# K and V laid out and fetched two heads at a time in a fused block-sparse attention and MoE kernel

## The chip, the cores and the metric

The kernel runs on one core of one Trainium2 chip. The metric is the device time of one execution, in microseconds (us). Of the kernel before three runs were timed: 549.1 us median (547.7 to 552.0).

## The reference

Attention over 4 batches, 8 heads, 768 tokens and 64 columns a head, in blocks of 32 tokens: a query block sees its neighbours, the first and the last block, and three blocks drawn at random for it (`sampled_blocks`). The first and last query blocks see everything. A top-1 mixture of 8 experts follows.

```python
scores = scale * np.matmul(q, k.transpose(0, 1, 3, 2))       # masked to window, first, last, sampled blocks
attn = np.exp(scores - max); attn = attn / (sum + 1e-9)
x = np.matmul(attn, v) -> (3072 tokens, 512)
e = argmax(x @ w_gate);  out = gate * sigmoid(x @ w_output_gate)[e] * (relu(x @ w1[e]) @ w2[e])
```

## The kernel before

The four batches are taken two at a time ("pairs of batches", `bp` 0 and 1): the two batches lie in the two halves of the partitions. One pass over a pair has `PER` = 26 steps. The first 4 steps are **dense** (class `Dense`): the first and the last query block of two heads (`u` and `u + 4`), against all 24 blocks of K. The 22 steps behind are **sparse** (class `Sparse`): 11 pairs of query blocks times two groups of four heads. The first experts' units run beside the second pass, the others after it.

K of one pair of batches is held as `kn`, 24 blocks of 256 columns (8 heads of 32 tokens), V as `vn`, six pieces of 128 tokens with all heads. For a pair of query blocks a tile `kr` (three in turn) collects 12 scaled K blocks: two copied by POOL once per `kr` (`fixed`, L410), four by DVE (`window_k`, L438), six drawn by number (`gather_k`, L421), of which ACT copies one and POOL five. Drawn V rows come by indirect DMA from POOL (`gather_v`, L448) with the row list `vidx`.

A step `n` runs, in program order on PE: the scores `pS` of step n, the output `pO` of step n-2 and the transposes `pT` of step n-1. DVE takes the row maxima (`dM`), ACT the exponentials (`aE`). A dense `pS` of step n+1 writes the score banks which the exponentials of step n read.

What else is to be issued is entered with `at(step, rank, function)` and runs at that step, in order of rank; each engine executes strictly in the order written. `spread` holds an SP transfer of ranks 3.3 and 3.6 in the first pass back to the step's first maximum or first ACT copy. The transfers of SP and ACT use eight semaphores in turn, so a transfer is issued only when the one eight before it has landed.

At the start PE runs warm-up matmuls on constants (`warm`, L172; their counts are in `NWARM`) until K is there. SP fetches the list of drawn blocks (`raw`, L193), K in two transfers of 12 blocks each (L395), V in six (L398), and then queries, V rows and gate weights. POOL and DVE make from `raw` the row list `vidx` (`setup_dup`, `setup_blocks`). A table in DRAM, by which experts find their tokens, is filled with a constant in four transfers (`fill`, L370) from a tile that POOL sets at step 3 (`setup_rest`). K of the second pair comes in 12 transfers (`LOAD_K`), its V in six (`LOAD_V`).

In the second pass SP also fetches expert weights in pieces of 512 KB (`load_w`, L983), which ACT (L1068) and DVE (L1072) split into two halves, and POOL gathers the tokens of the first units (`load_x`, L1010), which PE transposes (L1040).

Of the kernel before, what the change touches and what calls it, by code (L numbers as in the profile page):

```python
# [83 lines left out]
LOAD_K = 4, 5, 7, 9, 11, 13, 15, 17, 19, 21, 22, 23  # L84
# [17 lines left out]
NWARM = 44, 21, 11, 8, 8  # L102
# [16 lines left out]
def tile_kernel(ctx, tc, q, k, v, sampled, wg, wcat, out):  # L119
# [202 lines left out]
    def setup_blocks():  # L322
# [37 lines left out]
        nc.vector.tensor_copy(vidx[:, 1], tab)  # L360

    def setup_rest():
# [4 lines left out]
        for f in range(4):  # L367
            at(cur[0] + f, 3.3, fill, f, tz)
# [13 lines left out]
    vc = [ring.tile([128, 2, 8, VW], F32, name=f"vc{i}") for i in range(RC)]  # L382
# [38 lines left out]
    def gather_k(bp, i, kind, ns):  # L421
# [5 lines left out]
        for n, rv in zip(ns, regs):  # L427
            slot = n + 4 if n < 3 else n - 2
            if kind == "dve":
                nc.vector.tensor_single_scalar(r[:, slot:slot + 1], kn[bp][:, ds(rv, 1)], EXPS, op=ALU.mult)  # L430
            elif kind == "act":
                nc.scalar.activation(r[:, slot:slot + 1], kn[bp][:, ds(rv, 1)], AF.Copy, scale=EXPS)
            else:
                nc.gpsimd.tensor_tensor(  # L434
                    r[:, slot], kn[bp][:, ds(rv, 1)].rearrange("p o n -> p (o n)"), eighth.to_broadcast([128, 256]),
                    op=ALU.mult)

    def window_k(bp, i):  # L438
        a = 1 + 2 * i
        r = kr[i % RK]  # L440
        nc.vector.tensor_single_scalar(r[:, 0], kn[bp][:, a + 2], EXPS, op=ALU.mult)
        nc.vector.tensor_single_scalar(r[:, 7:10], kn[bp][:, a - 1:a + 2], EXPS, op=ALU.mult)

    def window_v(bp, i):
        a = 769 * bp + 32 + 64 * i
        spread(nc.sync.dma_start(vc[i % RC][0:64].rearrange("p b j w -> p (b j w)"), v[a:a + 64]))

    def gather_v(bp, i, s):  # L448
        if s == 0:
            vt[bp, i] = ring.tile([128, 2, 2, 8, VW], F32, tag="vt", name=f"vt{bp}_{i}", bufs=RV)  # L450
        behind(nc.gpsimd.indirect_dma_start(  # L451
            vt[bp, i][:, s].rearrange("p b j w -> p (b j w)"), None, v,
# [54 lines left out]
    class Sparse:  # L507
# [7 lines left out]
        def pS(self):  # L515
# [5 lines left out]
            for hp in range(2):  # L521
                for h2 in range(2):
                    for qi in range(2):
                        for b in range(2):
                            j = 4 * h2 + 2 * hg + hp
                            p = slice(64 * b, 64 * b + 64)
# [3 lines left out]
                                g[p, 1 - qi:3:1 + qi, :, 32 * j:32 * j + 32], start=True, stop=True)  # L530
# [19 lines left out]
        def pO(self):  # L550
# [3 lines left out]
            for b in range(2):  # L554
                for hp in range(2):
                    for h2 in range(2):
                        for qi in range(2):
# [4 lines left out]
                                av[:, qi, b, 4 * h2 + 2 * hg + hp], start=b == 0 and hp == 0, stop=False)  # L562
            for b in range(2):
                for hp in range(2):
                    for h2 in range(2):
# [954 lines left out]
```

## Time and profile before

| | |
|---|---|
| median of 3 runs | 549.1 us (547.7 to 552.0) |
| profiled execution, its own time | 543.43 us |
| its span | 541.8 us |
| busy share of PE, DVE, ACT, POOL | 94%, 66%, 57%, 46% |
| mean granted TensorE clock | 0.991 |

Times in rows are microseconds from the start of the span. PE is TensorE's matmuls, PEld its weight loads, DVE VectorE, ACT ScalarE, POOL GpSimd, SPq and POOLq the instructions that issue transfers. `[3.67 <-DMA x]` says that the engine was idle for 3.67 us before this instruction and what ended the idleness. The profiled execution is 5.7 us shorter than the median of the timed runs.

### The profile page before, as it was taken

What the parts mean: (1) busy time and instruction counts of PE and PEld (TensorE: products, weight loads), DVE (VectorE), ACT (ScalarE), POOL (GpSimd) and SP (SyncE); (2) the same over time, 40 slices, a digit from 0 to 9 for tenths busy, and PEclk for the clock granted to TensorE, in tenths of its full rate; (3) what the DMA queues carried; (4) which work ended last, traced back from release to release, by engine and by line L of the source; (5) the groups of instructions that cost most, each with busy time, mean ns of one, the idle gap of its engine ahead of it and who ended that gap; (6) DMA issues with size and microseconds to landing.
All of it is one profiled execution on the core that took longest, in us unless ns stands there. A gap on an engine that the chain in (4) does not pass through costs nothing. (4 is left out here: it accounts for less than half of the span.)

```text
span 541.8 us, 18874 instructions
## 1 busy us (share of the span) xinstructions
PE 510.1 (94%) x7429; PEld 358.9 (66%) x7429; DVE 357.3 (66%) x732; ACT 311.5 (57%) x584; POOL 249.0 (46%) x369
## 2 busy tenths in 40 slices
PE   8999999988879999999999999999999999999993
PEld 5466676666557667776777766677666667676671
DVE  5568577585679766876876668776755754465580
ACT  1455666665666656776666555666562663554480
POOL 3466566752755855548646337553421503211120
PEclk9999999999998999999999999999999999999997
DMA  7969988889399769887767595599998999996111
GB/s 295 280 197 306 294 259 264 237 239 298 92 327 311 202 224 301 242 230 251 220 209 227 142 343 197 203 391 402 405 301 299 325 399 313 301 326 232 28 40 37
DMA packets 60062, 137.98 MB, mean 255 GB/s; under 512 B 20471, under 2 KB 27131, under 8 KB 59708
## 3 DMA queue, kind: packets, MB, share of 16 engines
q1 hardware_dynamic: 48524, 99.93, 57.0%
q0 software_dynamic: 11296, 36.49, 21.1%
q8 instruction: 60, 0.98, 0.7%
q10 hardware_dynamic: 144, 0.26, 0.2%
q14 instruction: 38, 0.31, 0.2%
HBM read 127.88 MB, written 14.81 MB: 263 GB/s over the span
## 5 line engine op out<-in xcount | busy, mean ns | idle before, releaser
L1086 PE MATMUL h<-xb,kr 128*128 128x256 f16 (+1 forms) x780 | 86.9, 261 | 1.4 <-DMA xb<-xb 1.4
L1118 PE MATMUL S<-kr,hh 128*128 128x512 f16 x348 | 85.4, 379 | 0.0
L1086 PEld LDWEIGHTS <-kr 128*128 128x128 f16 x780 | 69.5, 98 | 19.7 <-issue 2.8
L434 POOL TENSOR_TENSOR kr<-kn,eighth 128x256 f32<-128x256 f32 x110 | 68.7, 651 | 9.1 <-issue 7.1
L534 DVE TENSOR_REDUCE mx<-S 128x4 f32<-128x1024 f32 x44 | 53.7, 1219 | 28.1 <-PE S L527 16.6
L542 ACT ACTIVATE P<-S,mx 128x256 f32<-128x256 f32 x176 | 69.1, 484 | 1.1 <-DVE mx L534 1.0
L451 POOL DMA_INDIRECT vt<-in_v_dram,vidx x44 | 45.0, 1022 | 51.5 <-DVE den L504 29.0
L1118 PEld LDWEIGHTS <-hh 128*128 128x128 f16 x384 | 36.9, 98 | 30.4
L493 ACT COPY pt<-T 128x512 f32<-128x512 f32 x66 | 36.9, 592 | 31.0 <-PE T L490 28.6
L1099 ACT ACTIVATE hh<-h 128x512 f16<-128x512 f32 (+1 forms) x36 | 19.7, 548 | 55.9 <-PE h L1086 55.4
L1010 POOL DMA_INDIRECT xb<-xscr,tab x16 | 20.7, 1295 | 63.0 <-issue 23.6
L527 PE MATMUL S<-kr,qall 64*32 64x256 f32 x1408 | 49.5, 386 | 0.0
L490 PE MATMUL T<-ident,P 128*128 128x128 f32 x352 | 46.0, 274 | 0.0
L1072 DVE SCALAR_TENSOR_TENSOR kr<-e,kr 128x1024 f16<-128x1024 f32 x32 | 38.3, 1219 | 9.8 <-ACT kr L1068 9.8
L804 POOL DMA_INDIRECT table<-vals,place x24 | 26.7, 1114 | 33.1 <-DVE den L504 21.1
L490 PEld LDWEIGHTS T<-ident,P 128*128 128x128 f32 x352 | 40.1, 143 | 1.6 <-issue 1.3
L560 PE MATMUL O<-vt,pt 128*32 128x65 f32 x1408 | 32.8, 222 | 4.7 <-issue 4.1
L1105 DVE SCALAR_TENSOR_TENSOR hh<-h,hh 128x512 f16<-128x512 f32 (+1 forms) x36 | 22.5, 626 | 19.7 <-ACT hh L1099 16.6
L1072 DVE SCALAR_TENSOR_TENSOR ws<-e,ws 128x1024 f16<-128x1024 f32 x24 | 29.9, 1246 | 7.0 <-PE h L1086 4.3
L560 PEld LDWEIGHTS O<-vt,pt 128*32 128x32 f32 x1408 | 25.6, 110 | 13.0 <-issue 8.8
L1086 PEld LDWEIGHTS <-ws 128*128 128x128 f16 x324 | 29.9, 99 | 5.4 <-issue 0.4
L1068 ACT ACTIVATE kr<-e 128x1024 f16<-128x1024 f32 x32 | 33.1, 1050 | 0.0
(349 smaller groups left out, 972.5 us busy)
## 6 DMA issues: line engine op xcount, KB each, us to landing
e<-in_wcat_dram SPq DMA_DIRECT2D x80, 512.0 KB
rk<-in_wcat_dram SPq DMA_DIRECT2D x30, 512.0 KB
vc<-in_wcat_dram SPq DMA_DIRECT2D x14, 512.0 KB
vn<-in_v_dram SPq DMA_DIRECT2D x12, 520.0 KB
xscr<-x SPq DMA_DIRECT2D x48, 128.0 KB
qall<-in_q_dram SPq DMA_DIRECT2D x23, 256.0 KB
vc<-in_v_dram SPq DMA_DIRECT2D x22, 260.0 KB
ws<-in_wcat_dram SPq DMA_DIRECT2D x8, 512.0 KB
```

The source lines that it names most:

```text
L434: nc.gpsimd.tensor_tensor(r[:, slot], kn[bp][:, ds(rv, 1)].rearrange("p o n -> p (o n)"), eighth.to_broadcast([128, 256]), op=ALU.mult)
L451: behind(nc.gpsimd.indirect_dma_start(vt[bp, i][:, s].rearrange("p b j w -> p (b j w)"), None, v, bass.IndirectOffsetOnAxis(ap=vidx[:, bp, ...
L490: nc.tensor.transpose(pt[:, 128 * c:128 * c + 128], p[:, 128 * c:128 * c + 128], ident)
L493: mark("copy", nc.scalar.copy(t[:, 0:w], pt[:, 0:w]))
L527: nc.tensor.matmul(s[64 * h2 + 32 * qi:64 * h2 + 32 * qi + 32, b, hp], t[p, 64 * j + 32 * qi:64 * j + 32 * qi + 32], g[p, 1 - qi:3:1 + qi, ...
L534: mark("max", nc.vector.tensor_reduce(mx, self.s.rearrange("p b h n -> p (b h) n"), axis=AX.X, op=ALU.max, negate=True))
L542: nc.scalar.activation(p[:, 256 * hp:256 * hp + 256], self.s[:, b, hp], AF.Exp, bias=self.mx[:, 2 * b + hp:2 * b + hp + 1])
L560: nc.tensor.matmul(o[row:row + 32, b, hp, 0:VW], self.t[b][:, col:col + 32], av[:, qi, b, 4 * h2 + 2 * hg + hp], start=b == 0 and hp == 0, ...
L1068: nc.scalar.activation(w[:, 0], piece(n), AF.Copy, scale=SW)
L1072: nc.vector.scalar_tensor_tensor(w[:, 1], piece(n), SW, w[:, 0], op0=ALU.mult, op1=ALU.subtract)
L1086: nc.tensor.matmul(hps[n // 2][:, cols(n)], w[:, hl, 128 * c:128 * c + 128], x[:, xl, c], start=cnt == 0, stop=cnt == 11)
L1118: nc.tensor.matmul(y, a[:, k], w[:, l, 512:1024], start=n % 8 == 0 and cnt == 0, stop=n % 8 == 7 and cnt == 2)
```

## The change

The columns of K are reordered in DRAM and in `kn`: the slowest index is now the pair of heads `u`, u + 4 (four "parts"), then the block, then 64 columns. V's rows are reordered in the same way. K of the first pair of batches comes in four transfers of one part each (768 KB), and the first of them stands ahead of `raw` on SP. V comes in twelve: the two first parts of all six pieces, then, behind the last part of K, the two others. Copies of single K blocks read or write four runs of 64 columns.

`setup_blocks` becomes a generator of four pieces, which run before step 0 and in steps 0, 1 and 2. `tz` is set on POOL before step 0, and the table's fills stand at steps 2 and 3. 30 of the warm-up matmuls with 512 columns go (one group of 11, and 19 of another's 21); the two groups of 8 in step 1 stay. The 12 transfers of the second K go to other steps, now by part and 8 blocks. In the second pass the fixed V rows (`fixed_v`) stand at steps 3, 5, 7 of the pass instead of 2, 3, 4, and the weight pieces of the first unit are fetched one step later.

```diff
-LOAD_K = 4, 5, 7, 9, 11, 13, 15, 17, 19, 21, 22, 23
+LOAD_K = 3, 3, 4, 5, 13, 15, 17, 19, 20, 21, 22, 23
-NWARM = 44, 21, 11, 8, 8
+NWARM = 44, 2, 8, 8
...
         for f in range(4):
-            at(cur[0] + f, 3.3, fill, f, tz)
+            at(2 + f // 2, (3.3, 3.6)[f % 2], fill, f, tz)
...
-    def load_k(bp, c):
-        spread(nc.sync.dma_start(kn[bp][:, c], k[bp, :, c]))
+    def load_k(bp, u, c):
+        spread(nc.sync.dma_start(
+            kn[bp][:, u, c].rearrange("p c x -> p (c x)"), k[bp, :, u, c].rearrange("p c x -> p (c x)")))
...
+    def parts(t):
+        return t.rearrange("p (u x) -> p u x", u=4)
...
             else:
                 nc.gpsimd.tensor_tensor(
-                    r[:, slot], kn[bp][:, ds(rv, 1)].rearrange("p o n -> p (o n)"), eighth.to_broadcast([128, 256]),
-                    op=ALU.mult)
+                    parts(r[:, slot]), block(bp, rv), eighth.unsqueeze(2).to_broadcast([128, 4, 64]), op=ALU.mult)
...
-        nc.vector.tensor_single_scalar(r[:, 7:10], kn[bp][:, a - 1:a + 2], EXPS, op=ALU.mult)
+        nc.vector.tensor_single_scalar(
+            r[:, 7:10].rearrange("p c (u x) -> p u c x", u=4), kn[bp][:, :, a - 1:a + 2], EXPS, op=ALU.mult)
...
                         nc.tensor.matmul(
                             self.s[b][64 * h2:64 * h2 + 64, half, 0:384], t[p, 64 * j:64 * j + 64],
-                            kn[bp][p, 12 * half:12 * half + 12, 32 * j:32 * j + 32], start=True, stop=True)
+                            kn[bp][p, u, 12 * half:12 * half + 12, 32 * h2:32 * h2 + 32], start=True, stop=True)
...
     load_q(0, NPAIR)
+    load_k(0, 0, slice(0, NB))
     setup_load()
     setup_dup()
-    load_k(0, slice(0, 12))
-    load_k(0, slice(12, 24))
+    load_k(0, 1, slice(0, NB))
+    load_k(0, 2, slice(0, NB))
...
     for c in range(6):
-        load_v(0, c)
+        load_v(0, c, slice(0, 2))
+    load_k(0, 3, slice(0, NB))
+    for c in range(6):
+        load_v(0, c, slice(2, 4))
...
-    setup_blocks()
+    blocks = setup_blocks()
+    next(blocks)
+    for n in range(3):
+        at(n, 3, next, blocks)
+    setup_rest()
...
-    at(3, 3, setup_rest)
...
-            at(o + (3 if bp == 0 else 2) + r, 3, fixed_v, bp, r)
+            at(o + (3 + r if bp == 0 else 3 + 2 * r), 3, fixed_v, bp, r)
...
-                    do(max(p - 5, (-3, 5, 5, 15)[u]), 0.6, load_w, n)
+                    do(max(p - (5 if u else 4), (-3, 5, 5, 15)[u]), 0.6, load_w, n)
```

How the change moves instructions. SP's queue from its first transfer on, before:

```order
L193 DMA raw<-in_sampled_dram 128x144
L395 DMA kn_224<-in_k_dram 128x3072 x2
L398 DMA vn_225<-in_v_dram 128x1040 x6
L404 DMA qall<-in_q_dram 128x512
L417 DMA vc_206<-in_v_dram 32x1040 x2
```

and with the change:

```order
L401 DMA kn_205<-in_k_dram 128x1536
L193 DMA raw<-in_sampled_dram 128x144
L401 DMA kn_205<-in_k_dram 128x1536 x2
L406 DMA vn_206<-in_v_dram 128x520 x6
L401 DMA kn_205<-in_k_dram 128x1536
L406 DMA vn_206<-in_v_dram 128x520 x6
L414 DMA qall<-in_q_dram 128x512
L430 DMA vc_187<-in_v_dram 32x1040 x2
```

The first part of K now goes ahead of the list of blocks, the last part goes behind half of V.

DVE's queue at the first two dense steps, with the change (before, all the rows on `sf`, `t`, `wf`, `tab` and `vidx` stood ahead of the first maximum; `mx0d_0` is the first maximum of step 0, `pt0d_0` a copy of its transposes):

```order
L336 SCALAR_TENSOR_TENSOR bad<-dd,bad 128x72
L616 TENSOR_REDUCE mx0d_0_293<-S_75 128x1
L616 TENSOR_REDUCE mx1d_0_295<-S_76 128x1
L340 TENSOR_SCALAR sf<-sf,rf 128x72
L344 TENSOR_TENSOR sf<-sf,t_277 128x72
L616 TENSOR_REDUCE mx1d_1_330<-S_76 128x1
L511 COPY pt1d_0_342<-T1d_0_338 128x384
L349 CAST wf<-wi 128x22
L350 TENSOR_SCALAR wf<-wf,rf 128x22
L456 TENSOR_SCALAR kr_184<-kn_205 128x256
L457 TENSOR_SCALAR kr_184<-kn_205 128x4x3x64
L616 TENSOR_REDUCE mx0d_2_449<-S_75 128x1
```

(Rows between them are left out.) The third piece of the lists stands between the copies of step 0 and the window's copies into `kr`, which stand ahead of step 2's maximum.

SP's queue at the start of the second pass, before (`e` are weight pieces, `vc` V rows):

```order
L987 DMA e_3450<-in_wcat_dram 128x1024
L417 DMA vc_206<-in_v_dram 32x1040 x2
L446 DMA vc_206<-in_v_dram 64x1040
L404 DMA qall<-in_q_dram 128x512
L987 DMA e_3450<-in_wcat_dram 128x1024
L417 DMA vc_207<-in_v_dram 32x1040 x2
```

and with the change:

```order
L1002 DMA e_3428<-in_wcat_dram 128x1024
L462 DMA vc_187<-in_v_dram 64x1040
L414 DMA qall<-in_q_dram 128x512
L1002 DMA e_3428<-in_wcat_dram 128x1024
L430 DMA vc_187<-in_v_dram 32x1040 x2
```

Ahead of the first row stand two more weight pieces before and one with the change; the fixed V rows (32x1040, two at a time) go behind the next weight piece.

## Rows read from the trace of the kernel before

**Rows 1.** The page's first part: busy time, share of the span, instructions.
```profile
PE 510.1 (94%) x7429; PEld 358.9 (66%) x7429; DVE 357.3 (66%) x732; ACT 311.5 (57%) x584; POOL 249.0 (46%) x369
```

**Rows 2.** Waits of PE: engine, line, waited for; us in total, times, longest.
```profile
PE O L1040 <- DMA e<-xscr,tab: 2.9, 2, 2.0
```

**Rows 3.** Timeline of the first 35 us, all engines: start, us, engine, line.
```profile
1.72 9.56 PE L175 MATMUL O<-ones,ones 128*128 128x128 f16 x65 [1.72 <-DVE eighth L181]
...
6.45 0.63 ACT L408 ACTIVATE qall<-qall 128x512 f32<-128x512 f32 x1 [3.67 <-DMA qall<-in_q_dram]
6.62 0.19 DVE L323 COPY smp<-raw 1x72 int32<-1x72 int32 x1 [3.24 <-DMA raw<-in_sampled_dram]
...
7.04 0.27 POOL L229 TENSOR_TENSOR dupd<-dupf 128x48 f32<-128x48 f32 x1
...
7.38 0.27 POOL L230 TENSOR_TENSOR dupd<-dupd 128x48 f32<-128x48 f32 x1
...
7.92 0.23 DVE L336 SCALAR_TENSOR_TENSOR bad<-dd,bad 128x72 f32<-128x72 f32 x1
...
10.14 0.17 DVE L347 CAST wf<-wi 128x22 f32<-128x22 int32 x1
...
11.63 0.17 DVE L355 COPY tab<-sf 32x11 f32<-32x11 f32 x1
...
12.60 0.18 DVE L360 CAST vidx<-tab 128x22 int32<-128x22 f32 x1
...
14.04 0.61 POOL L412 TENSOR_TENSOR kr<-kn,eighth 128x256 f32<-128x256 f32 x1 [3.03 <-DMA kn<-in_k_dram]
...
15.42 0.96 DVE L601 TENSOR_REDUCE mx0d<-S 128x1 f32<-128x768 f32 x1 [2.64 <-PE S L593]
...
19.48 1.19 POOL L412 TENSOR_TENSOR kr<-kn,eighth 128x256 f32<-128x256 f32 x2
...
22.95 0.55 DVE L442 TENSOR_SCALAR kr<-kn 128x768 f32<-128x768 f32 x1
...
23.37 1.52 PE L593 MATMUL S<-kn,qall 64*64 64x384 f32 x16
...
25.00 0.96 DVE L601 TENSOR_REDUCE mx0d<-S 128x1 f32<-128x768 f32 x1 [1.49 <-ACT kr L432]
...
30.15 0.96 DVE L601 TENSOR_REDUCE mx0d<-S 128x1 f32<-128x768 f32 x1 [1.58 <-PE S L593]
...
33.65 1.09 PE L527 MATMUL S<-kr,qall 64*32 64x256 f32 x32
```

**Rows 4.** Stretches: busy us of each engine, then granted clock, DMA share, GB/s.
```profile
0.00:6.45 6.45, 4.74 (x45) 4.84 (x46) 2.27 (x20) 1.49 (x2) 2.43 (x17) 1.00 0.54 161
0.00:8.25 8.25, 6.54 (x52) 5.60 (x53) 3.82 (x29) 2.11 (x3) 3.73 (x23) 1.00 0.64 219
0.00:14.04 14.04, 12.32 (x83) 7.95 (x84) 7.11 (x48) 2.11 (x3) 5.27 (x28) 1.00 0.78 300
0.00:17.85 17.85, 15.82 (x101) 9.07 (x102) 8.93 (x50) 3.56 (x7) 8.23 (x33) 1.00 0.83 325
```

**Rows 5.** Stretches later on; columns PE, PEld, DVE, ACT, POOL as above.
```profile
55.00:60.00 5.00, 3.71 (x100) 2.83 (x99) 2.22 (x6) 3.08 (x8) 3.04 (x4) 1.00 1.01 309
160.50:162.85 2.35, 0.32 (x4) 0.11 (x2) 2.28 (x7) 2.12 (x5) 0.00 (x0) 1.00 1.02 279
164.00:167.30 3.30, 3.30 (x68) 2.49 (x54) 3.22 (x6) 1.05 (x2) 1.92 (x3) 0.51 1.03 263
```

**Rows 6.** Timeline at the start of the second pass.
```profile
153.13 0.99 POOL L1010 DMA_INDIRECT e<-xscr,tab  x1 [0.72 <-DVE dend L504]
...
162.85 0.63 PE L1040 MATMUL O<-ident,e 128*128 128x128 f32 x4 [2.04 <-DMA e<-xscr,tab]
...
171.10 0.97 DVE L442 TENSOR_SCALAR kr<-kn 128x768 f32<-128x768 f32 x1
```

**Rows 7.** Groups of instructions: line, engine, shapes, count, busy us, mean ns.
```profile
L434 POOL TENSOR_TENSOR kr<-kn,eighth 128x256 f32<-128x256 f32 x110 | 68.7, 651 | 9.1 <-issue 7.1 <-PE S L527 1.3
```

More of the change, by code (lines that the diff above doesn't have):

```diff
@@ L351, in setup_blocks @@
         for g in range(4):
+            if g == 2:
+                yield
             pp = slice(32 * g, 32 * g + 32)
@@ L360, in setup_blocks @@
         nc.vector.tensor_copy(vidx[:, 1], tab)
+        yield
     def setup_rest():
@@ L381, in tile_kernel @@
     kr = [ring.tile([128, 12, 256], F32, name=f"kr{i}") for i in range(RK)]
-    vc = [ring.tile([128, 2, 8, VW], F32, name=f"vc{i}") for i in range(RC)]
+    vc = [ring.tile([128, 4, 2, 2, VW], F32, name=f"vc{i}") for i in range(RC)]
     qall = ring.tile([128, RQ, 512], F32, name="qall")
@@ L388, in prep_alloc, with load_v @@
     def prep_alloc(bp):
-        kn[bp] = big.tile([128, NB, 256], F32, tag="kn", name=f"kn{bp}", bufs=2)
+        kn[bp] = big.tile([128, 4, NB, 64], F32, tag="kn", name=f"kn{bp}", bufs=2)
     def prep_alloc_v(bp):
-        vn[bp] = big.tile([128, 6, 2, 8, VW], F32, tag="vn", name=f"vn{bp}", bufs=1)
-    def load_k(bp, c):
-        spread(nc.sync.dma_start(kn[bp][:, c], k[bp, :, c]))
-    def load_v(bp, c):
-        spread(nc.sync.dma_start(vn[bp][:, c].rearrange("p b j w -> p (b j w)"), v[769 * bp + 128 * c:769 * bp + 128 * c + 128]))
+        vn[bp] = big.tile([128, 6, 4, 2, 2, VW], F32, tag="vn", name=f"vn{bp}", bufs=1)
+    def load_k(bp, u, c):
+        spread(nc.sync.dma_start(
+            kn[bp][:, u, c].rearrange("p c x -> p (c x)"), k[bp, :, u, c].rearrange("p c x -> p (c x)")))
+    def load_v(bp, c, us=slice(0, 4)):
+        n = VROW // 4
+        spread(nc.sync.dma_start(
+            vn[bp][:, c, us].rearrange("p u b h w -> p (u b h w)"),
+            v[769 * bp + 128 * c:769 * bp + 128 * c + 128, n * us.start:n * us.stop]))
     qt, vt = {}, {}
@@ L412, in fixed @@
             nc.gpsimd.tensor_tensor(
-                kr[r][:, 10 + j], kn[bp][:, 23 * j], eighth.to_broadcast([128, 256]), op=ALU.mult)
+                parts(kr[r][:, 10 + j]), kn[bp][:, :, 23 * j], eighth.unsqueeze(2).to_broadcast([128, 4, 64]), op=ALU.mult)
     def fixed_v(bp, r):
@@ L440, in window_k @@
         r = kr[i % RK]
-        nc.vector.tensor_single_scalar(r[:, 0], kn[bp][:, a + 2], EXPS, op=ALU.mult)
-        nc.vector.tensor_single_scalar(r[:, 7:10], kn[bp][:, a - 1:a + 2], EXPS, op=ALU.mult)
+        nc.vector.tensor_single_scalar(parts(r[:, 0]), kn[bp][:, :, a + 2], EXPS, op=ALU.mult)
+        nc.vector.tensor_single_scalar(
+            r[:, 7:10].rearrange("p c (u x) -> p u c x", u=4), kn[bp][:, :, a - 1:a + 2], EXPS, op=ALU.mult)
     def window_v(bp, i):
         a = 769 * bp + 32 + 64 * i
-        spread(nc.sync.dma_start(vc[i % RC][0:64].rearrange("p b j w -> p (b j w)"), v[a:a + 64]))
+        spread(nc.sync.dma_start(vc[i % RC][0:64].rearrange("p u b h w -> p (u b h w)"), v[a:a + 64]))
     def gather_v(bp, i, s):
         if s == 0:
-            vt[bp, i] = ring.tile([128, 2, 2, 8, VW], F32, tag="vt", name=f"vt{bp}_{i}", bufs=RV)
+            vt[bp, i] = ring.tile([128, 2, 4, 2, 2, VW], F32, tag="vt", name=f"vt{bp}_{i}", bufs=RV)
         behind(nc.gpsimd.indirect_dma_start(
-            vt[bp, i][:, s].rearrange("p b j w -> p (b j w)"), None, v,
+            vt[bp, i][:, s].rearrange("p u b h w -> p (u b h w)"), None, v,
             bass.IndirectOffsetOnAxis(ap=vidx[:, bp, i, s:s + 1], axis=0)).ins)
@@ L529, in pS @@
                                 t[p, 64 * j + 32 * qi:64 * j + 32 * qi + 32],
-                                g[p, 1 - qi:3:1 + qi, :, 32 * j:32 * j + 32], start=True, stop=True)
+                                g[p, 1 - qi:3:1 + qi, :, n:n + 32], start=True, stop=True)
         def dM(self):
@@ L561, in pO @@
                                 o[row:row + 32, b, hp, 0:VW], self.t[b][:, col:col + 32],
-                                av[:, qi, b, 4 * h2 + 2 * hg + hp], start=b == 0 and hp == 0, stop=False)
+                                av[:, qi, 2 * hg + hp, b, h2], start=b == 0 and hp == 0, stop=False)
             for b in range(2):
@@ L568, in pO @@
                             o[64 * h2:64 * h2 + 64, b, hp, 0:VW], self.t[b][:, col:col + 64],
-                            cv[:, b, 4 * h2 + 2 * hg + hp], start=False, stop=b == 1 and hp == 1)
+                            cv[:, 2 * hg + hp, b, h2], start=False, stop=b == 1 and hp == 1)
         def fin(self):
@@ L628, in pO @@
                             o[64 * h2:64 * h2 + 64, b, 0, 0:VW], t[:, col + 64 * h2:col + 64 * h2 + 64],
-                            vn[bp][:, c, b, 4 * h2 + u], start=b == 0 and c == 0, stop=b == 1 and c == 5)
+                            vn[bp][:, c, u, b, h2], start=b == 0 and c == 0, stop=b == 1 and c == 5)
         def fin(self):
@@ L931, in piece @@
             pool4["k"] = big.tile([128, 6, 1024], F32, tag="kn", name="rk", bufs=2)
-        v = [t.rearrange("p b j w -> p (b j w)")[:, 0:1024] for t in vc]
+        v = [t.rearrange("p u b h w -> p (u b h w)")[:, 0:1024] for t in vc]
         a, b = early_buffers(0), early_buffers(1)
@@ L1408, in tile_kernel @@
         if step == 1:
-            warm(3, 512)
+            warm(2, 512)
         enters = isinstance(now, Dense) and isinstance(last, Sparse)
@@ L1423, in tile_kernel @@
                 if step == 1:
-                    warm(4, 512)
+                    warm(3, 512)
                 now.aE()
```

25 lines of the change are left out of this document (14 added, 11 removed).

## Prediction

> **What bounds the kernel now.** First the page: PE is busy 94% of the span [rows 1], so what the kernel loses it loses where PE has no work. The waits of PE name only one large transfer, the gathered tokens of the second pass [rows 2]. But at the start the warm-up matmuls count as work: 65 of them run back to back from 1.72 us [rows 3], and they compute nothing. So the second view is the timeline of the first 35 us. There the first row maximum starts at 15.42, at the end of DVE's wait for the scores [rows 3], and the scores had waited for K, whose second half POOL has at 14.04 [rows 3]. Until then the transfers bound the kernel. Third, the stretches: how much has been moved by when, and where else PE idles. [...]
>
> **When a transfer lands.** By 6.45 us 161 GB/s x 6.45 = 1.04 MB have moved, and q and `raw` (262 and 74 kB) have landed [rows 3, 4]: 0.70 MB more than they hold. By 14.04 it is 300 x 14.04 = 4.21 MB, for q, `raw` and all of K (3.48 MB): 0.73 more [rows 3, 4]. So I take a transfer as landed when 0.72 MB more than it and those ahead of it have moved. K's first part (786 kB) behind q: 0.26 + 0.79 + 0.72 = 1.77 MB; at 8.25 us 219 x 8.25 = 1.81 MB [rows 4], so **8.2 us**. `raw` comes 0.2 us later, at 8.4 instead of 6.6. The second part: 10.2. The last part, behind half of V: q, `raw`, four parts and 1.60 MB of V are 5.08 MB, with 0.72 it is 5.80; at 17.85 us 325 x 17.85 = 5.80 [rows 4], so **17.85 us**. The second half of V: 1.6 MB later, below 22.
>
> **The change, part by part.**
>
> *First scores.* q is on ACT's queue and now shares the engines with K's first part instead of the small `raw`. It lands between its own 6.45 and 8.2, and 0.63 us of scaling [rows 3] follow: 7.1 to 8.9, I take 8.5. The 16 matmuls of a dense step take 1.52 us [rows 3], so they end at 10.0. DVE's first list piece, 6.62 to 8.15 [rows 3], runs from 8.4 to 10.0 and is just out of the way. The first maximum starts at 10.1 instead of 15.42: **5.3 us earlier** (4.9 to 6.7). The second part of K (10.2) is there when the exponentials free the banks, the third at about 12.
>
> *Warm-ups.* The 30 matmuls cost nothing: PE waits for K there. Their cover gone, PE idles from about 7 (45 matmuls are done by 6.45, one or two remain [rows 4]) to 8.5.
>
> *Lists on DVE.* The second piece (five operations) fits between the maxima of steps 0 and 1, as POOL's part of the list, 1.8 us later with `raw`, is done by 11.5. The third piece, 10.14 to 11.63, so 1.5 us [rows 3], stands between step 0's copies and the window copies. DVE's idle time ahead of step 2's maximum is 1.49 us [rows 3], so it just fits. The fourth piece (11.63 to 12.78, 1.15 us) goes into a gap of 1.58 [rows 3]. So the lists alone cost about 0. But the window's two copies need K's last part (17.85), and POOL, which did its copies from 14.04 to 20.67 beside a mostly idle DVE [rows 3], now does them from 17.85 on, beside the window's. The large window copy takes 0.55 us at 22.95 [rows 3] and 0.97 at 171.10 beside POOL's copies [rows 6]: 0.42 for it, about 0.2 for the small one. I take **0.6 us later** (0.2 to 1.4: the upper end if the last part of K comes at the 309 GB/s of [rows 5] from 14.04 on, at 19.2). [...]
>
> *POOL.* Its copies end 6.6 us [rows 3] after 17.85, at 24.5, those for the first sparse step before that. That step started at 33.65 [rows 3] and would now start at 29: 4.5 us to spare. The setting of the table's tile moves ahead of them, into POOL's wait for K; 0. The row list is ready at about 25, when POOL reaches the gather of V rows; 0.
>
> *Copies in four runs.* The shapes' sizes stay; 0, see the last rival.
>
> *Table, second K.* Four fills (1.77 MB) leave the stretch from 32 to 49 us for about 20 to 28, when SP's queue stood still before; four K pieces are fetched by step 5. So there is less traffic from 35 to 65, where PE idled 1.29 us in five [rows 5]. I take **0.5 us gained** (0 to 1.3). SP's row for the fill now waits for step 2's maximum, with only later transfers behind it; 0.
>
> *Second pass.* The gather of tokens issued at 153.13 holds PE until 162.85 [rows 6], 9.7 us, with the engines full. Ahead of it or beside it, one weight piece (524 kB) and four fixed V transfers (532 kB) go later: 1.06 MB, 3.8 us at 279 GB/s [rows 5], of which the gather's queue gets a part. PE's wait is 2.04, and half of 3.3 us at the lower clock is 1.65 [rows 2, 5]; so at most 3.7 us. But DVE is busy 2.28 of the 2.35 us of this wait [rows 5] and comes late next. I take **1.0 us gained** (0 to 3.7). Pieces of weights that come a step later have over 12 us between transfer and use.
>
> *Sum.* -5.3 + 0.6 - 0.5 - 1.0 = **-6.2 us**. The profiled execution took 543.4 us by its own time (span 541.8), so 537.2 by this sum. The median of the timed runs is 549.1, 5.7 us higher for reasons that this profile cannot show; taking the same 6.2 off gives **542.9 us**.
>
> **Rivals.**
>
> *The second pass gives all.* If PE's wait and the clock's fall both go (3.7), the middle gives 1.3 and the start 4.9, it is 9.9: **539**. For it: the transfers are full there; against: DVE is too. Chance 0.10.
>
> *Half the lead is lost at the start.* The first part of K lands near 9.5 (the early rate of the rows is the least sure number), or PE, now idle from 7, drops to the lower clock: then the 1.52 us of step 0 and those of step 1 take twice as long, some 3 us. 2.5 to 3.5 us less: **545.5**. For it: an idle 2.35 us preceded the fall in [rows 5]. Against it: the gap here is some 1.5 us. [...] Chance 0.20.
>
> *POOL's late start eats it.* POOL begins 3.8 us later than before (17.85 against 14.04). If the sparse steps hang on its queue, copies and gathers of V rows in turn, only 0 to 2 us are left: **548.5** (546.5 to 550.5). Against it: the 4.5 us to spare. Chance 0.11.
>
> *POOL's copies get slower: the other side.* 110 copies at 651 ns [rows 7] now read and write four runs of 64 instead of one of 256. POOL is busy 3.04 of 5 us [rows 5], some 2.4 of it such copies, so it is full when a copy takes 1.8 times as long, 1.2 us. From there each 0.1 us costs 110 x 0.1 = 11 us: at 1.35 us it is 16 - 6, so **559**. Against it: on POOL 24 runs of 2 numbers took 0.27 us, as much as 48 in one run [rows 3]. Chance 0.07.
>
> That the change does not do what it says is out: each part of K is a transfer of its own, and by the order of instructions the first scores wait for one.
>
> **How the numbers follow.** My forecast, 5 to 7.7 us less, has 0.52; 541.4 to 544.1. A measurement of this kernel tells 1%, 5.5 us, from no change: faster means below 543.6, slower above 554.6. Of the forecast 0.42 lies below 543.6, with the first rival's 0.10 this is 0.52 for faster. Same: 0.10 + 0.20 + 0.11 = 0.41. Slower: 0.07. The range reaches from 538.5, the first rival, to 548.5; it leaves out the last rival and half of the one before it.
>
> **What would show it.** In the profile after: the first maximum near 10.1 us (if at 12, the rate or the clock); K's last part on POOL at 17.9; step 2's maximum near 20.3; the first sparse scores near 29.0; POOL's copies still near 651 ns; PE's wait for the gathered tokens under 1 us and no fall of the clock at 160. If the first sparse scores start before 29.5 and the time is still above 545, the later terms are wrong: the lead was given back, and PE's waits must name the place.

## The result, and the profile after

| | kernel before | with the change | ratio, 95% interval |
|---|---|---|---|
| first comparison, 4 runs each | 549.6 us | 542.9 us | 0.9894 (0.9850 to 0.9938) |
| second, another chip, 35 and 12 runs | 537.0 | 535.9 | 0.9983 (0.9945 to 1.0021) |
| third, another chip, 35 and 12 runs | 548.8 | 543.7 | 0.9918 (0.9885 to 0.9951) |
| fourth, another chip, 35 and 12 runs | 548.9 | 544.7 | 0.9941 (0.9906 to 0.9976) |

The first row is the result that the forecast stood against: 542.9 us, as forecast. The other three came with the experiments. Times the median, the ratios are 5.8 us less (3.4 to 8.2), 0.9 (-1.1 to 3.0), 4.5 (2.7 to 6.3) and 3.2 (1.3 to 5.2); the mean of the four is 3.6. Three of the four intervals exclude 1, so the change makes the kernel faster, but by less than the sum's 6.2 us: only the first comparison lies in the forecast range of 5 to 7.7 us less. The ratios, and the mean times and clocks below, leave out runs more than 1.5% longer than the fastest of their kernel; the medians take in all.

The two profiles at hand cannot show this: the span is 541.5 us after and was 541.8 before. The profiled execution of before (543.43 us) is quicker than every one of the 74 timed runs of it in the comparisons where its median is 548.8 us or more. So stretches are compared below, not ends. First the page after, to be set beside [rows 1, 7].

```profile
span 541.5 us, 18824 instructions
...
PE 504.1 (93%) x7399; PEld 356.2 (66%) x7399; DVE 359.0 (66%) x732; ACT 311.9 (58%) x584; POOL 249.2 (46%) x369
...
DMA  8999889897299689878776594699998999996111
...
L450 POOL TENSOR_TENSOR kr<-kn,eighth 128x256 f32<-128x256 f32 x110 | 70.2, 665 | 7.4 <-issue 6.8
```

PE has 30 matmuls less, and POOL's copies take 665 ns in place of 651. The start, timelines of PE, then DVE, then POOL (start, us, engine, line):

```profile
6.92 1.52 PE L608 MATMUL S<-kn,qall 64*64 64x384 f32 x16
...
11.40 2.46 PE L608 MATMUL S<-kn,qall 64*64 64x384 f32 x16 [1.13 <-ACT P01d L625]
...
29.05 1.09 PE L544 MATMUL S<-kr,qall 64*32 64x256 f32 x32
```
```profile
7.87 0.18 DVE L323 COPY smp<-raw 1x72 int32<-1x72 int32 x1 [4.49 <-DMA raw<-in_sampled_dram]
...
9.31 0.95 DVE L616 TENSOR_REDUCE mx0d<-S 128x1 f32<-128x768 f32 x1
...
18.78 0.97 DVE L457 TENSOR_SCALAR kr<-kn 128x768 f32<-128x768 f32 x1
19.67 0.95 DVE L616 TENSOR_REDUCE mx0d<-S 128x1 f32<-128x768 f32 x1
...
23.10 0.61 DVE L360 COPY tab<-sf 32x11 f32<-32x11 f32 x1
23.73 0.56 DVE L359 COPY tab<-wf 32x11 f32<-32x11 f32 x1
```
```profile
18.72 1.50 POOL L425 TENSOR_TENSOR kr<-kn,eighth 128x256 f32<-128x256 f32 x2 [7.06 <-DMA kn<-in_k_dram]
```

The scores start at 6.92, right behind the warm-ups and without a wait, so K's first part had landed by then, at least 1.3 us before the forecast landing. They end at 8.44; the first maximum waits until 9.31 behind the list's first piece, which `raw` releases only at 7.87. It was at 15.42 [rows 3]. Step 2's maximum is at 19.67, the first sparse scores start at 29.05 (33.65 before): the lead is 4.6 us, as the sum had it by there.

Further on, the stretches of 21 to 56 us, before and then after (columns as in [rows 4]):

```profile
21.00:28.00 7.00, 6.67 (x86) 4.04 (x84) 5.37 (x11) 5.30 (x11) 0.00 (x0) 1.00 0.65 116
...
35.00:42.00 7.00, 6.60 (x145) 5.33 (x140) 4.74 (x11) 2.34 (x7) 6.05 (x33) 1.00 0.91 265
42.00:49.00 7.00, 6.19 (x164) 4.63 (x165) 6.04 (x21) 5.12 (x13) 3.58 (x5) 1.00 0.98 317
```
```profile
21.00:28.00 7.00, 4.95 (x78) 3.25 (x76) 6.80 (x17) 3.83 (x9) 6.64 (x11) 1.00 1.07 274
...
35.00:42.00 7.00, 7.00 (x167) 5.84 (x169) 6.31 (x21) 3.25 (x8) 5.19 (x8) 1.00 1.04 247
42.00:49.00 7.00, 4.76 (x130) 3.27 (x126) 5.05 (x13) 3.58 (x10) 3.27 (x5) 1.00 1.03 333
```

The transfers, which had a lull (0.65) while SP's queue stood still, now have a share of 0.99 to 1.07 through 49 us, and PE, busy 6.19 of 7 us in 42 to 49 before, is busy 4.76. Taken at the first scores of the same sparse step, the lead is 4.6 to 5.1 us up to 47 us, 2.9 at 56, and 4.3 again at 61, since the kernel before pauses a little later; it is 4.7 at 97, 3.9 at 125 and 0.7 at 296. So in this pair most of it goes behind 97 us, in pieces of up to 1.2 us.

At the start of the second pass (waits of PE; timeline; stretch) nothing of what the forecast promised is seen:

```profile
PE O L1055 <- DMA e<-xscr,tab: 2.1, 1, 2.1
```
```profile
159.52 0.63 PE L1055 MATMUL O<-ident,e 128*128 128x128 f32 x4 [2.14 <-DMA e<-xscr,tab]
```
```profile
159.50:161.66 2.16, 2.14 (x36) 1.08 (x36) 1.70 (x3) 1.96 (x3) 1.81 (x2) 0.62 1.04 311
```

PE waits 2.14 us, 2.04 before [rows 6], and the granted clock falls again (0.62 over this stretch, 0.50 from 160.1 to 161.66). The 0.8 us that the tokens cost before that [rows 2] is gone, but the lead does not grow: 3.9 us at 125, 3.4 at 170.

### The profile page after: what moved, and what is told of

Its sections match the earlier page's. It is cut to its first block, busy times and chain, and to the rows that moved or that the text cites. A ratio compares the mean times of both kernels' runs of the same rounds, so it can differ in the third digit from the quotient of the medians.

```text
span 541.5 us, 18824 instructions
## 1 busy us (share of the span) xinstructions
PE 504.1 (93%) x7399; PEld 356.2 (66%) x7399; DVE 359.0 (66%) x732; ACT 311.9 (58%) x584; POOL 249.2 (46%) x369
## 5 line engine op out<-in xcount | busy, mean ns | idle before, releaser
L450 POOL TENSOR_TENSOR kr<-kn,eighth 128x256 f32<-128x256 f32 x110 | 70.2, 665 | 7.4 <-issue 6.8
L467 POOL DMA_INDIRECT vt<-in_v_dram,vidx x44 | 44.1, 1003 | 44.3 <-DVE den L520 30.5
L577 PE MATMUL O<-vt,pt 128*32 128x65 f32 x1408 | 33.1, 222 | 4.7 <-issue 4.2
L584 PE MATMUL O<-vc,pt 128*64 128x65 f32 x704 | 32.0, 229 | 2.6 <-issue 2.6
L577 PEld LDWEIGHTS O<-vt,pt 128*32 128x32 f32 x1408 | 25.8, 109 | 13.0 <-issue 7.7
```

Source lines behind the costliest of these rows:

```text
L450: nc.gpsimd.tensor_tensor(parts(r[:, slot]), block(bp, rv), eighth.unsqueeze(2).to_broadcast([128, 4, 64]), op=ALU.mult)
L467: behind(nc.gpsimd.indirect_dma_start(vt[bp, i][:, s].rearrange("p u b h w -> p (u b h w)"), None, v, bass.IndirectOffsetOnAxis(ap=vidx[:, ...
L577: nc.tensor.matmul(o[row:row + 32, b, hp, 0:VW], self.t[b][:, col:col + 32], av[:, qi, 2 * hg + hp, b, h2], start=b == 0 and hp == 0, stop ...
L584: nc.tensor.matmul(o[64 * h2:64 * h2 + 64, b, hp, 0:VW], self.t[b][:, col:col + 64], cv[:, 2 * hg + hp, b, h2], start=False, stop=b == 1 a ...
```

## The experiments

Four kernels on each of three chips, each beside 35 runs of the kernel before. Every one left a trace, and the lead over a trace of the kernel's old start can be read from it. Theory A: the head start is the gain.

**The change again, parts of it, and the warm-ups back.** `e1_again` is the change unedited.

> The change once more, unedited, beside the kernel before. Theory A (the head start is the gain): the first scores come 6 us sooner, 4.6 us of it stands at the first sparse step, and it is carried to the end one for one; the pair of traces at hand, in which the lead shrinks from 4.6 us at step 4 to 0.5 us at 298 us, is a quick execution of before against a common one of the change. Then the time is again 542 to 544 beside 548 to 550, and a second trace of the change keeps its lead where the first one lost it, in other places at least. Rival B (the lead is eaten): later waits that belong to the change use it up, as that pair shows; then the ratio is nearer to 1 (0.995 to 1) and the second trace loses the lead at the same places, by 0.7 to 1.2 us each.

`e2_start_only`:

```diff
-LOAD_K = 3, 3, 4, 5, 13, 15, 17, 19, 20, 21, 22, 23
+LOAD_K = 4, 5, 7, 9, 11, 13, 15, 17, 19, 21, 22, 23
-            at(o + (3 + r if bp == 0 else 3 + 2 * r), 3, fixed_v, bp, r)
+            at(o + (3 if bp == 0 else 2) + r, 3, fixed_v, bp, r)
-                    do(max(p - (5 if u else 4), (-3, 5, 5, 15)[u]), 0.6, load_w, n)
+                    do(max(p - 5, (-3, 5, 5, 15)[u]), 0.6, load_w, n)
```

> The change with its later parts undone: the second K pieces, the fixed V transfers and the first weight piece of the second pass are at their old steps; layout, K and V two heads at a time, lists in four parts and the early table stay. Theory A: 0 to 1 us slower than the change, 542.9 to 544, since PE's wait for the gathered tokens was 2.0 us before and is 2.1 us after it. Rival C (the later parts give the gain): 3 us or more of the 6.8 us are lost, 546 to 549.

`e3_late_only`, on the kernel before:

```diff
-            at(o + (3 if bp == 0 else 2) + r, 3, fixed_v, bp, r)
+            at(o + (3 + r if bp == 0 else 3 + 2 * r), 3, fixed_v, bp, r)
-                    do(max(p - 5, (-3, 5, 5, 15)[u]), 0.6, load_w, n)
+                    do(max(p - (5 if u else 4), (-3, 5, 5, 15)[u]), 0.6, load_w, n)
```

> The kernel before, with two of the later parts alone: the fixed V transfers of the second pair two steps apart, and the first weight piece one step later. Theory A: within 1 us of before, 548.5 to 550; PE still waits about 2 us for the gathered tokens and the clock still falls after it. Rival C: 3 us or more faster, 543 to 546.

`e4_warm_back`:

```diff
-NWARM = 44, 2, 8, 8
+NWARM = 44, 21, 8, 8
```

> The change with 19 more warm-up matmuls of 512 columns (21 in place of 2) ahead of the first scores, so that PE comes to them some 4 us later (19 x 0.21 us) although K has landed; nothing else moves. Theory A: the first row maximum goes from 9.3 to about 12.9 us and the time goes up by the same 3.6 us, to 546.5 (545 to 547.5). Rival B (what is won at the start is eaten later): 0 to 1 us, 543 to 544. If PE's clock suffers from its pause before the first scores in the change, the loss is smaller than 3.6 us, and the scores of step 0 are quicker than in the change.

Measured:

| | median us | ratio to before (95%) | mean us | mean clock |
|---|---|---|---|---|
| before | 537.0 | | 535.8 | 0.9919 |
| e1_again | 535.9 | 0.9983 (0.9945 to 1.0021) | 535.8 | 0.9867 |
| e2_start_only | 536.3 | 0.9994 (0.9952 to 1.0036) | 535.9 | 0.9873 |
| e3_late_only | 535.1 | 1.0012 (0.9980 to 1.0043) | 535.5 | 0.9914 |
| e4_warm_back | 537.6 | 0.9994 (0.9952 to 1.0035) | 536.9 | 0.9896 |

Rival C falls: the second pass and the second pair's K undone (e2), or the second pass's two parts alone (e3), move nothing that can be told (e2 less e1 0.1 us in the means, -1.8 to 2.0; e3 less before -0.3, -1.7 to 1.1). In the trace of e3 PE still waits there, 0.8 us for the tokens and then 1.3 for DVE:

```profile
PE O L1040 <- DVE e L1047: 1.3, 1, 1.3
...
PE O L1040 <- DMA e<-xscr,tab: 0.8, 1, 0.8
```

Theory A in its simple form falls too. e1's first maximum comes at 9.42 us and its first sparse scores at 29.95 (33.33 in e3), and yet it gains about 1 us, a ratio in rival B's range of 0.995 to 1. And e4, whose first maximum comes 3.4 us later (12.77), is only 1.1 us slower than e1 in the means (-0.8 to 3.0): less than the lead that it gives away, and not to be told from nothing. The last column has another side of it. In the kernel before, 12 matmuls of a dense V product (L627) start 0.65 us apart at a clock of 0.50 (165.70 and 166.35 us) and 0.35 us apart at 1.00 (35.07 and 35.42). Taken as twice the time at half the clock, an estimate, a mean clock of 0.9867 in place of 0.9919 is 0.0052 x 537 = 2.8 us lost. Putting the warm-ups back raises the clock by 0.0029 (-0.0002 to 0.0060), 1.6 us, which these runs do not tell from nothing either. A stretch of the trace of e1 (its longest run of twelve, 542.5 us) and its PE rows show one place where the clock is lost:

```profile
12.47:15.88 3.41, 3.41 (x17) 1.44 (x18) 0.49 (x2) 0.00 (x0) 0.00 (x0) 0.50 1.05 411
```
```profile
8.06 1.90 PE L175 MATMUL O<-ones,ones 128*128 128x512 f16 x8
11.51 3.78 PE L608 MATMUL S<-kn,qall 64*64 64x384 f32 x16 [1.55 <-ACT P01d L625]
```

Behind idle stretches up to 11.51 us the granted clock is at 0.50 for 3.41 us, and the scores of step 1 take 3.78 us instead of the 2.46 above. Of seven traces with the change's own warm-ups three have this fall (e1, e2, and f3 below) and lose 1.4 us by it until 24 us; of five with more of them none has. But these falls are the smaller part. Over the seven traces a low clock costs up to 0.7 us a trace before 30 us, 1.2 from 30 to 130 (with falls at 45 to 47 us in three of them, at a pause of PE) and 3.2 from 130 to 200, where the two traces of the old start (before, e3) lose 0, 0 and 1.7 us each. POOL's copies take as long in the one layout as in the other on this chip, 683 and 684 ns; e1's row, and e3's with the old layout:

```profile
L450 POOL TENSOR_TENSOR kr<-kn,eighth 128x256 f32<-128x256 f32 x110 | 72.3, 683 | 7.3 <-issue 6.1 <-PE T L506 0.4 <-PE O L584 0.2
```
```profile
L434 POOL TENSOR_TENSOR kr<-kn,eighth 128x256 f32<-128x256 f32 x110 | 72.4, 684 | 9.9 <-issue 7.1 <-PE O L567 2.0 <-PE O L1086 0.2
```

**PE's pauses in the middle.** Most pauses of PE between 30 and 300 us are put down to "issue", nothing that the profile shows. But the DMA table of the change's page (part 3) has this queue:

```profile
q8 instruction: 60, 0.98, 0.7%
```

These are 60 transfers of 16 KB, one for every 247 of PE's 14,800 matmuls and weight loads. Over all fourteen traces there are 60 such pauses of more than 0.6 us in these 270 us: 48 of them end 1.20 to 1.65 us after one of these transfers has ended (a moment picked at random has a chance of 6% for that). Of the other 12, eleven are at one place (`route_p` L695, L680 before, at 44 to 49 us), treated below. Worked out from the traces, the pause in the first V product (L577, 32 matmuls) behind that place:

```
trace              16 KB transfer ended   PE's pause ended   pause   behind L577's
after              44.45                  45.85              0.77    15th matmul
e1_again           45.53                  46.96              2.02    15th
f4 (the change)    44.41                  45.68              1.04    15th
h4 (the change)    43.67                  45.09              0.45    15th
f1 (2 warm-ups)    44.48                  45.79              1.05    13th
h2 (4 warm-ups)    44.90                  46.36              0.97    11th
h1 (index later)   43.37                  44.64              1.81    30th
h3 (both)          44.32                  45.79              2.36    26th
before             45.68                  (no pause)
e3_late_only       44.11                  (no pause)
```

In the last column the pause goes by the count of PE's matmuls, not by what they compute. In all eight rows with a pause it stands behind the 600th matmul of the program, whichever matmul that is: with two or four more warm-ups it comes two or four matmuls earlier within L577, and with the 15 matmuls of `setup_index` (L304) run later, in h1, 15 matmuls later. (e2 and f3 have it behind the 15th as well, with 0.49 and 1.17 us.) And 47 of the 48 pauses stand at this place or whole steps of 126 to 127 matmuls behind it; of the other 12 none does. The queue's name, the count and the 1.20 to 1.65 us are what the traces show. That PE's own instructions come in these transfers, and late, is read from them; no view shows what PE waits for.

With the old start PE came to this place 3 to 5 us later, when the transfer had ended, and did not pause; with the new one it comes first and pauses. Theory D made this the place where the head start is paid, since the DMA share is 1.03 there (42 to 49 us).

`f1_k_first`:

```diff
     load_q(0, NPAIR)
-    load_k(0, 0, slice(0, NB))
     setup_load()
     setup_dup()
+    load_k(0, 0, slice(0, NB))
...
+    load_k(0, 3, slice(0, NB))
     for c in range(6):
         load_v(0, c, slice(0, 2))
-    load_k(0, 3, slice(0, NB))
...
-NWARM = 44, 2, 8, 8
+NWARM = 44, 2, 10, 8
```

> The change with its first transfers in another order: the list of blocks ahead of K's first part, K's last part ahead of V's first half; two more warm-up matmuls of 512 columns between the scores of steps 0 and 1. Theory D (the transfers stand at their limit from 7 to 49 us in the change, PE's own instructions come late through them, and the head start pays for it there): the first maximum at 8.7 instead of 9.3, K's last part at 14.5 to 16 instead of 18.5, PE's pauses of 21 to 28 us fall from 1 to 2 us to some 0.5, but those of 42 to 49 stay at 2 to 2.5, so 0.5 to 1.5 us faster than the change. Rival E (the head start is lost to DVE's and POOL's collision before 28 us alone): the pauses of 42 to 49 go too and it is 2 to 3 us faster.

`f2_quiet_middle`, besides:

```diff
-LOAD_K = 3, 3, 4, 5, 13, 15, 17, 19, 20, 21, 22, 23
+LOAD_K = 12, 13, 14, 15, 16, 17, 18, 19, 20, 21, 22, 23
-            at(2 + f // 2, (3.3, 3.6)[f % 2], fill, f, tz)
+            at(6 + f, 3.6, fill, f, tz)
```

> As f1_k_first, and the table's four fills four steps later (6 to 9), the first four pieces of the second pair's K at steps 12 to 16 in place of 3 to 5: 2.8 MB less in the stretch of 22 to 49 us. Theory D: the DMA share of 28 to 42 falls below 0.9, PE's pauses of 42 to 49 fall to 1 us or less, the lead over the kernel before at 56 us is 4.5 to 5.5 us, and the time is 1.5 to 3 us below the change. Rival E: as f1_k_first, within 0.7 us. Rival F (what is moved away comes back between 50 and 120 us, where the share is 0.8 to 1.0 already): the lead at 56 us is there, but shrinks to 2 or 3 us by 130, and the time is that of the change.

`f3_more_traffic`:

```diff
         at(LOAD_K[n], 3.3, load_k, 1, n // 3, slice(8 * (n % 3), 8 * (n % 3) + 8))
+        if n < 4:
+            for more in (2, 4):
+                at(LOAD_K[n] + more, 3.3, load_k, 1, n // 3, slice(8 * (n % 3), 8 * (n % 3) + 8))
```

> The change with the first four pieces of the second pair's K fetched three times in place of once, each again two and four steps later: 2.1 MB more between 35 and 70 us, 6 us of transfers at 330 GB/s, and nothing else. Theory D: PE's pauses between 42 and 70 us grow by 2 to 5 us and the time by 1.5 to 5 us. Rival G (PE bounds the middle, and its pauses there are chance): 0 to 1 us.

`f4_change_again`, unedited:

> The change once more, unedited, to set the other three against on their own chip, and a third trace of it. Both theories: the lead at step 4 is 3.5 to 5 us again, it loses 1 us or more between 40 and 50 us, PE pauses 2 us or more there; and the ratio to the kernel before lies between the two measured so far, 0.989 and 0.998. Where a pause of PE has no wait in the profile and comes from its own instructions arriving late, it ends 1.2 to 1.6 us after one of the sixty 16 kB instruction transfers.

| | median us | ratio to before (95%) | mean clock | us in pauses that end 1.2 to 1.65 us behind a 16 KB transfer, 30 to 300 us |
|---|---|---|---|---|
| before | 548.8 | | 0.9911 | 2.5 (first profile) |
| f4_change_again | 543.7 | 0.9918 (0.9885 to 0.9951) | 0.9887 | 2.7 |
| f3_more_traffic | 545.1 | 0.9932 (0.9897 to 0.9967) | 0.9883 | 4.5 |
| f2_quiet_middle | 548.0 | 0.9974 (0.9932 to 1.0015) | 0.9854 | 9.6 |
| f1_k_first | 548.7 | 0.9976 (0.9934 to 1.0017) | 0.9864 | 5.2 |

The last column is of one execution each; those of f2 and f3 (552.2 and 547.6 us) are the longest of their twelve.

f1 missed: 3 to 5 us slower than the change, where 0.5 to 1.5 us less was expected. The order of two transfers explains 0.7 of it:

```profile
8.44 1.52 PE L608 MATMUL S<-kn,qall 64*64 64x384 f32 x16 [2.33 <-DMA kn<-in_k_dram]
```

With the list (74 kB, one row for all partitions) ahead of it, K's first part lands at least 1.5 us later than with the change (by 6.92), and the first maximum is at 10.00 in place of 9.31. The rest goes with the lower clock (0.0023 x 548 = 1.3 us) and the pauses behind 16 KB transfers (2.5 us more), and what makes these more frequent here is not shown. Rival E falls too: the pause of 42 to 49 us is still there (1.05 us). f2 moved the pause and brought no gain. Its stretches, columns as before:

```profile
35.00:42.00 7.00, 6.74 (x157) 5.65 (x153) 5.73 (x21) 3.01 (x8) 4.68 (x7) 1.00 0.82 229
42.00:49.00 7.00, 6.17 (x181) 4.44 (x179) 6.02 (x14) 5.01 (x13) 3.82 (x6) 1.00 0.63 199
49.00:56.00 7.00, 3.93 (x46) 2.83 (x44) 1.00 (x4) 2.22 (x5) 3.26 (x5) 0.76 1.01 331
```
```profile
52.47 0.69 PE L678 MATMUL O<-ident,x 128*128 128x128 f32 x2 [3.07 <-issue]
```

Where the share is 0.63, PE is busy 6.17 us and the pause in the V product is gone; the 16 KB transfer had ended at 42.41. In the next seven us the share is 1.01, the next such transfer ends at 51.06, and PE pauses 3.07 us, until 52.47. So rival F had the direction right, the pause moves to where the share is 1.01, but not the numbers: the lead over the kernel before is 0.9 us at 56, not 4.5 to 5.5, it is 3.6 us behind at 125, and the time is 3 to 5 us above the change's. f3, with 2.1 MB more, has 1.8 us more of such pauses and 1.3 us more time (1.7 in the means, 0.3 to 3.1), at the lower end of what D expected and just above rival G's. In f4 what both theories expected is seen: the ratio between the two, the lead of 5.4 us at step 4 (3.5 to 5 expected) down to 2.5 at 57 us. But the kernel before pauses a little later, 1.3 us at 59, and by 66 us the lead is 3.9 again, so D's place costs 1.5 us of lead and not the head start.

**A collision, and a filled gap.** At L695 PE goes on 0.10 us after DVE has read a bank of outputs, in f4 and in the change's first profile alike. Its pause, 1.43 and 1.47 us, which the profile puts down to "issue", is read from this as a wait for that bank. The row of f4 (PE follows at 43.99):

```profile
43.47 0.42 DVE L521 TENSOR_TENSOR x<-O,den 128x256 f32<-128x256 f32 x1
```

Ahead of it one of DVE's small index operations takes 1.97 us beside POOL's copies; DVE and POOL of the change's first profile:

```profile
38.63 1.97 DVE L313 CAST pf<-pb 128x2 f32<-128x2 int32 x1
```
```profile
38.81 1.75 POOL L450 TENSOR_TENSOR kr<-kn,eighth 128x256 f32<-128x256 f32 x3
```

In the trace before the same operation took 0.22 us, though POOL ran three such copies there too:

```profile
44.18 0.22 DVE L313 CAST pf<-pb 128x2 f32<-128x2 int32 x1
```
```profile
43.19 1.76 POOL L434 TENSOR_TENSOR kr<-kn,eighth 128x256 f32<-128x256 f32 x3 [0.26 <-issue]
```

So not every operation takes longer there; which one does, and by how much, is not shown. `h1_index_later`:

```diff
-    at(5, 3, setup_index)
+    at(8, 3, setup_index)
```

> The change with the setting of the index tables (twelve small operations on DVE, one bank on PE) at step 8 in place of step 5, nothing else. In the traces of the change one of these operations is held 1.3 to 2.0 us beside POOL's copies at 38 to 40 us, and PE then pauses 1.4 us at 43 for a bank that DVE frees late. Theory C (part of the head start is paid at this collision): the pause at 43 falls below 0.6 us, the lead at 47 us is 0.8 to 1.5 us larger, and the time 0.5 to 1.5 us lower than the change's. Rival (the same operations cost as much at step 8): a pause of 1 us or more 15 us later, no difference in time.

`h2_warm_gap`:

```diff
-NWARM = 44, 2, 8, 8
+NWARM = 44, 2, 12, 8
```

> The change with four more warm-up matmuls of 512 columns between the scores of steps 0 and 1, 0.95 us, in a pause of 1.1 to 1.5 us in which PE waits for ACT's exponentials. In three of five traces with the change's own start the clock falls at 12.5 us for 3.4 us, right behind that pause, and costs 1.4 us until 24 us; in those with the pause filled it does not. Theory K (the warm-ups that the change took out held the clock up): no fall at 12.5 us, the mean granted clock of the timed runs 0.001 to 0.002 higher than the change's, and the time 0.5 to 1 us lower. Rival: the falls at the start have another cause, the clock and the time stay.

`h3_both` has both edits.

> Both edits at once, as the version that the traces point to: four more warm-up matmuls in the pause behind step 0's scores, and the index tables at step 8. Theories C and K together: 1 to 2.5 us below the change, and 5 to 8 us below the kernel before on a chip where the change gains 4.5, 2 to 3.5 on one where it gains 1. Rival (what is won up to 50 us is lost to PE's late instructions and the clock behind it): within 0.7 us of the change.

`h4_change_third` is the change unedited.

> The change unedited, to set the other three against on their own chip. If the gain over the kernel before hangs on the chip, a chip on which the kernel before takes 545 us or more gives 0.989 to 0.992, one on which it takes 540 or less 0.995 to 1; if the two ratios so far differ by chance alone, it is 0.993 to 0.996 on either.

| | median us | ratio to before (95%) | mean clock |
|---|---|---|---|
| before | 548.9 | | 0.9907 |
| h4_change_third | 544.7 | 0.9941 (0.9906 to 0.9976) | 0.9872 |
| h1_index_later | 544.3 | 0.9944 (0.9911 to 0.9978) | 0.9895 |
| h2_warm_gap | 545.3 | 0.9942 (0.9904 to 0.9981) | 0.9874 |
| h3_both | 544.2 | 0.9950 (0.9917 to 0.9984) | 0.9865 |

None beats the change. h1 took the collision's pause away and PE lost it again 2.5 us later, in the pause behind the 600th matmul; PE in f4 (the change) and then in h1:

```profile
43.99 0.42 PE L695 MATMUL O<-xT,wst 128*32 128x128 f32 x8 [1.43 <-issue]
44.21 0.43 PE L577 MATMUL O<-vt,pt 128*32 128x65 f32 x15
45.68 0.58 PE L577 MATMUL O<-vt,pt 128*32 128x65 f32 x17 [1.04 <-issue]
```
```profile
41.95 0.42 PE L695 MATMUL O<-xT,wst 128*32 128x128 f32 x8
42.20 0.63 PE L577 MATMUL O<-vt,pt 128*32 128x65 f32 x30
44.64 0.27 PE L577 MATMUL O<-vt,pt 128*32 128x65 f32 x2 [1.81 <-issue]
```

Of the 1.43 us, 0.8 came back as a longer pause there, and h1 passes the place 1 us sooner than f4; in the time nothing is left of that. On h1's own chip h4 has 1.45 and 0.45 us at the two places, 1.90 against h1's 1.81. In h2 the pause behind step 0's scores is 0.41 us instead of 1.0 to 1.5, but the mean clock is 0.0002 higher, not 0.001 to 0.002; on this chip no trace of the unedited start shows the fall at 12.5, so there was nothing to win, and theory K is neither shown nor refuted by it. h4 gave 0.9941 on a chip where the kernel before takes 548.9 us: within what "chance alone" expected (0.993 to 0.996) and outside what "the chip decides" did (0.989 to 0.992), but its interval reaches into both. The first, third and fourth ratio agree within their intervals; the second chip's differs from the first and the third by more than chance easily gives, and these runs do not settle why.

## Why the prediction was right, step by step

**First scores, -5.3.** Right in size, by two errors that cancel: the first part of K landed by 6.9, not at 8.2 (the estimate with 0.72 MB fails this early), and the list's first piece, taken to be just out of the way, held the maximum until 9.3. Measured: 6.1 us at steps 0 and 1.

**Lists and window copies, +0.6.** Seen at 0.8 to 1.5 us: the lead is 5.3 at step 2 and 4.6 at the first sparse step in the first profile, 5.4 in those of f4 and h4. The large window copy took 0.97 us beside POOL as priced; the fourth list piece, priced at nothing, has three copies of 0.56 to 0.65 us beside POOL's instead of 0.16. So DVE took longer beside POOL's copies here and at the 1.97 us above, with the 0.22 us of that operation in the trace before as a reminder that an overlap is not always paid.

**Warm-ups, 0.** This step failed in part. They compute nothing, but with them gone three of seven traces have a fall of the clock at 12.5 us (1.4 us each, so 0.6 us a trace), and of five with some of them back none has. In e1 the clock is at 0.50 from 12.47 to 15.88 us, behind a pause of 1.55. The mean clock of the change is lower than that of the kernel before by 0.0052, 0.0024 and 0.0035 on three chips, 2.8, 1.3 and 1.9 us, and most of it is lost later. f1, f2, h2 and h3, with two or four warm-ups back and no fall at 12.5, have mean clocks of 0.9854 to 0.9874 where the change has 0.9887 and 0.9872, so the warm-ups are not shown to be its cause. A lower clock at the start was part of the second rival, half the lead lost there.

**POOL, copies in four runs.** 0 each, right: the first sparse scores came at 29.05 (28.2 to 30.0 in eleven traces), the copies' mean is that of the old layout on the same chip (683 and 684 ns), or 5 to 14 ns more on other chips (651 before, 656 to 665 after).

**Table and second K, -0.5.** Wrong in sign for 21 to 49 us: with the transfers moved up the DMA share of that stretch is 0.99 to 1.07, where it was 0.55 to 0.98. In its place stand PE's pauses behind the 16 KB transfers.

**Second pass, -1.0.** Nothing: e3's ratio is 1.0012 (0.9980 to 1.0043), and the wait and the clock's fall are still there. In e3 the tokens hold PE for less, but then DVE does (1.3 us), which the forecast had named as the limit of this term.

So the sum's first two terms, -4.7, are what the start gives (4.6 to 5.4 us at step 4, on the second comparison's chip 3.4 to 4.1 where the clock had fallen); the later -1.5 is not there. What was measured lies near the head start less the clock's extra loss: 5.0 less 2.8, 1.3 and 1.9 us is 2.2, 3.7 and 3.1, measured 0.9, 4.5 and 3.2. This is an account, not an experiment, and it leaves things out. The pauses behind 16 KB transfers take 4.1 us a trace with the change's own start (30 to 300 us, seven traces) and 2.5 and 0.8 in the two traces of the old one. e4 alone tests it, and does not contradict it (3.4 us later at the first maximum, 1.6 us of clock back, 1.1 us slower, -0.8 to 3.0). The first comparison does not fit it: its four runs have a mean clock of 0.9862 against 0.991 in the one run of before whose clock is on record, which would leave 2.4 us of 5.0, where 3.4 to 8.2 were measured. The closeness of 542.9 to the forecast is then partly luck: the two terms that gave nothing were worth 1.5 us of the sum, nothing in it stood for the clock or for the pauses behind the 16 KB transfers, and in the other three comparisons the gain is 0.9 to 4.5 us. What makes it differ so is open.

## What to carry over

A head start can be spent before the end: 5.4 us at step 4 ended as 4.5 and 3.2 (third and fourth comparison), and the 16 KB transfer of the table above ended at 43.4 to 45.5 us with the new start, at 44.1 and 45.7 with the old. Ask of every transfer ahead, those of the "instruction" queue among them, whether it comes earlier too. Warm-up work that fills a wait may not be free to remove: look at the clock behind the gap that it leaves, here 0.50 in three of seven traces. And where executions scatter by 1%, compare two profiles stretch by stretch and never by their ends.

## What the hardware showed that was not expected

A queue that the page calls "instruction" moves 60 transfers of 16 KB, and of PE's 60 pauses of more than 0.6 us between 30 and 300 us that fourteen traces put down to "issue" 48 end 1.20 to 1.65 us after one of them: 0.8 to 9.6 us in all, by trace. 47 of the 48 stand at counts of matmuls that are whole steps of 126 to 127 apart, whatever the matmul there computes.

A small DVE operation (128x2) beside three POOL copies took 1.97 us in one trace and 0.22 in another; three 32x11 copies beside POOL's took 0.56 to 0.65 instead of 0.16.

With a list of 74 kB for all partitions ahead of 786 kB of K the first scores waited for K until 8.44 us; in the other order they start at 6.92 without a wait.

The same kernel takes 537 us on one chip and 549 on two others. Short pauses within the V product (three or four of 0.4 to 0.5 us, 4.4 to 5.0 us apart, between 95 and 118 us, in the change and in the kernel before alike) are in all traces of the first, third and fourth comparison and in none of the second's, where POOL's copies in turn take 3% longer (684 ns); what they are is open.
